# 32x32 block inverses moved by VectorE transposes instead of through DRAM, and an opening in program order, in a DeltaNet and feed-forward kernel

## The chip, the cores and the metric

One core of one Trainium2 chip. The metric is the device time of one execution in microseconds (us). A kernel's time is the median of its runs. A ratio is the mean time of one kernel's fast runs over the mean of the other's fast runs of the same rounds, with a 95% interval, so it isn't quite the ratio of the medians quoted here.

## The reference, cut to what matters

Four batches of eight heads, 768 positions, head width 48: a linear attention whose state is corrected at every position. Its output, 3072 tokens of 384 numbers, goes through a feed-forward network of width 2048.

```python
for t in range(S):
    kt, vt, bt = (k_n[:, :, t], v[:, :, t], beta[:, :, t, None])
    y[:, :, t] = np.einsum('bhd,bhde->bhe', q[:, :, t], state)
    v_old = np.einsum('bhde,bhd->bhe', state, kt)
    state = state + bt[:, :, :, None] * np.einsum('bhd,bhe->bhde', kt, vt - v_old)
...
h = x @ w_in
g = np.maximum(h, 0.0) + alpha * np.minimum(h, 0.0)
return (g @ w_out).astype(np.float32)
```

The kernels cut the sequence into 12 chunks of 64 positions. With two pairs of batches that makes 24 steps. Within a chunk the recurrence is a triangular system of 64x64 for each head, solved with the inverses of its two 32x32 diagonal blocks. VectorE works these out by elimination, one block in each partition ("eliminate"), so a block that lies across 32 partitions has to be moved into one, and its inverse back. The weights arrive as 64-bit words and are turned into fp32 on the chip, piece by piece, by ScalarE, VectorE and GpSimd. A feed-forward "unit" is one chunk's tokens: a first half (times `w_in`, then PReLU) and a second half (times `w_out`).

## The kernel before

The blocks went through DRAM: an image of all blocks was stored, gathered into partitions, and after the elimination stored again and scattered.

```python
def gather(n):
    ...
    nc.sync.dma_start(out=image, in_=kk[n])
    for t in range(2):
        for i in range(2):
            ...
            nc.sync.dma_start(
                out=block[m][blocks_of(n, t, i)],
                in_=image[rows, :, HB * i : HB * i + HB].rearrange("r h c -> h r c"),
            )

def eliminate(m, eng):
    ...                                   # 60 operations on VectorE
    eng.tensor_copy(out=flipped[0:np_], in_=r.rearrange("p r c -> p c r"))
    nc.sync.dma_start(out=inverse[m][0:np_], in_=r)
    nc.sync.dma_start(out=turned[m][0:np_], in_=flipped[0:np_])

def scatter(n):
    ...
    for dst, src, i in (
        (diag[n % NE][first, :, 0:HB], turned[m], 0),
        (diag[n % NE][second, :, HB:C], inverse[m], 1),
        (inv[n % NE][first, :, 0:HB], inverse[m], 0),
    ):
        nc.sync.dma_start(out=dst, in_=src[blocks_of(n, t, i)].rearrange("h r c -> r h c"))
```

The weights' words were converted by one generator, and the order of instructions on each engine was the scheduler's:

```python
for i, (dst, _) in enumerate(pieces):
    ...
    nc.scalar.activation(dst.bitcast(U32), lo, ACT.Copy, scale=2.0**-29)
    nc.scalar.square(size, hi.bitcast(FP32))
    nc.vector...      # two operations: high, hi
    nc.gpsimd.tensor_tensor(out=dst.bitcast(U32), in0=hi, in1=dst.bitcast(U32), op=ALU.add)
    nc.vector...      # one operation: the check
    if i + len(stages) < len(pieces):
        fetch_words(i + len(stages))
```

## Time and profile before

| | kernel before |
|---|---|
| time (median of four runs; 844.66 is that of the three known at the prediction) | 844.2 us |
| the profiled run: time; span | 843.51 us; 841.7 us |
| opening, to the first full pair of steps | 211.9 us, PE busy 118.5 |
| ten pairs of steps | 584.2 us, PE busy 582.3 |
| the last unit | 45.6 us |

The stretch in the middle can be cut once more. The next view of the kernel before gives the busy time by stretches: window, its length, then busy us and number of instructions of PE, PEld, DVE, ACT and POOL, then the granted TensorE clock, the DMA share and GB/s. Steps 4 and 5 are the first line, steps 6 to 23 the second:

```profile
211.90:271.50 59.60, 59.38 (x760) 44.93 (x759) 37.28 (x102) 11.49 (x24) 1.21 (x5) 1.00 0.38 83
271.50:796.10 524.60, 522.89 (x6358) 392.76 (x6358) 217.33 (x567) 94.23 (x186) 4.51 (x22) 1.00 0.25 51
```

In both PE is busy all but 2 us. Whatever helps must act before 212 us, or take work away from PE.

### The profile page before, as it was taken

To read this page: it belongs to the slowest core of one execution; us is meant where nothing else is said; L and a number is where in the kernel's file an instruction comes from. 1 tells how busy PE (TensorE), PEld (TensorE's weight loads), DVE (VectorE), ACT (ScalarE), POOL (GpSimd) and SP (SyncE) were. 2 spreads that over 40 slices of the span, in tenths; PEclk is the share of its full clock that TensorE was granted. 3 is DMA by queue.
4 is the path that set the end of the run, shared out by engine and by line. 5 is a ranking of instruction groups with operands and counts; after the bars stand their busy time and mean duration, and the time that the engine had idled before them with its cause. 6 is when DMAs were issued, how large, how long until landed. Compare 5 with 4: busy or idle time off the path is not lost.

```text
span 841.7 us, 20438 instructions
## 1 busy us (share of the span) xinstructions
PE 742.2 (88%) x8917; PEld 558.1 (66%) x8917; DVE 388.8 (46%) x955; ACT 169.7 (20%) x318; POOL 53.8 (6%) x96
## 2 busy tenths in 40 slices
PE   4402686886999999999999999999999999999997
PEld 3301575653876876867867768768768768677684
DVE  3779764452592430881422943216818713123030
ACT  2231223222211211211302201211212112011010
POOL 5022121122000000000000000000000000000000
PEclk9999989997999999999999999999999999999999
DMA  5774074353325223314303232331333321100000
GB/s 104 196 201 130 18 105 140 102 146 74 72 40 137 46 44 74 58 69 78 66 25 63 59 104 43 57 58 43 85 58 58 61 48 21 23 11 2 20 1 19
DMA packets 178520, 58.06 MB, mean 69 GB/s; under 512 B 167920, under 2 KB 171008, under 8 KB 177664
## 3 DMA queue, kind: packets, MB, share of 16 engines
q1 hardware_dynamic: 177984, 56.65, 30.7%
q8 instruction: 70, 1.15, 0.6%
q10 hardware_dynamic: 448, 0.11, 0.1%
q14 instruction: 18, 0.15, 0.1%
HBM read 39.43 MB, written 17.30 MB: 67 GB/s over the span
## 4 chain that ended last, share of the span: by engine, by line
PE 79%; DVE 8%; issue 6%; POOL 3%; DMA 2%; SPq 1%; ACT 1%; DVEq 0%; POOLq 0%; ACTq 0%
PE p_ffn L536 29%; PE p_ffn L516 28%; PE p_one L464 3%; PE p_one L478 3%; PE p_one L411 3%; PE p_one L422 3%; PE p_big L309 3%; PE p_big L449 2%; PE p_big L282 2%; DVE prod L369 2%; POOL w_out L191 2%; DVE block L375 2%; DMA ke<-in_k_dram 1%; PE p_one L505 1%; PE p_big L484 1%
## 5 line engine op out<-in xcount | busy, mean ns | idle before, releaser
L536 PE MATMUL p_ffn<-w_out,g 128*128 128x384 f32 x768 | 270.2, 500 | 21.5 <-DVE w_out L192 20.5
L516 PE MATMUL p_ffn<-xt,w_in 128*128 128x256 f32 x1152 | 268.2, 386 | 3.1 <-ACT xt L506 2.5
L516 PEld LDWEIGHTS p_ffn<-xt,w_in 128*128 128x128 f32 x1152 | 215.2, 192 | 33.4 <-ACT xt L506 2.8
L536 PEld LDWEIGHTS p_ffn<-w_out,g 128*128 128x128 f32 x768 | 142.7, 193 | 112.4 <-DVE w_out L192 16.7
L527 DVE SCALAR_TENSOR_TENSOR g<-low,al_t,p_ffn 128x256 f32<-128x256 f32 x192 | 85.6, 477 | 130.6 <-ACT low L524 130.3
L524 ACT ACTIVATE low<-p_ffn 128x512 f32<-128x512 f32 x96 | 57.4, 598 | 174.2 <-PE p_ffn L516 165.9
L369 DVE TENSOR_TENSOR prod<-block 128x84 f32<-128x84 f32 (+22 forms) x210 | 70.8, 337 | 5.0
L375 DVE TENSOR_TENSOR block<-block,prod 128x84 f32<-128x84 f32 (+22 forms) x210 | 70.6, 336 | 4.9
L411 PE MATMUL p_one<-diag,kk 64*64 64x32 f32 x768 | 33.2, 226 | 28.4 <-DMA diag<-turned 28.3
L411 PEld LDWEIGHTS p_one<-diag,kk 64*64 64x64 f32 x768 | 29.3, 142 | 39.5 <-issue 37.6
L425 DVE TENSOR_TENSOR inv<-diag,p_one 128x256 f32<-128x256 f32 x24 | 10.1, 419 | 96.1 <-PE p_one L422 84.7
L543 ACT COPY o_sb<-p_ffn 128x384 f32<-128x384 f32 x24 | 11.5, 479 | 169.3 <-PE p_ffn L536 169.3
L452 DVE TENSOR_TENSOR r<-v_raw,p_big 128x384 f32<-128x384 f32 x22 | 12.1, 552 | 72.3 <-PE p_big L449 72.3
L422 PEld LDWEIGHTS p_one<-diag,mid 64*64 64x64 f32 x768 | 25.9, 142 | 13.0 <-ACT mid L414 8.2
L478 PEld LDWEIGHTS p_one<-u,a_t 64*64 64x64 f32 x768 | 25.8, 142 | 11.7 <-issue 8.2
L492 DVE TENSOR_TENSOR y<-y,p_one 128x384 f32<-128x384 f32 x22 | 12.2, 553 | 46.1 <-PE p_one L478 46.1
L422 PE MATMUL p_one<-diag,mid 64*64 64x32 f32 x768 | 28.4, 226 | 4.8 <-ACT mid L414 4.7
L478 PE MATMUL p_one<-u,a_t 64*64 64x48 f32 x768 | 28.9, 227 | 2.0 <-DVE u L466 2.0
L464 PEld LDWEIGHTS p_one<-r,inv 64*64 64x64 f32 x704 | 22.6, 134 | 10.4 <-issue 7.0
L271 POOL TENSOR_TENSOR beta_t<-beta_t,rec 128x8 f32<-128x8 f32 x24 | 7.4, 307 | 345.1 <-DVE rec L269 345.1
L414 ACT COPY mid<-p_one 128x256 f32<-128x256 f32 x24 | 8.9, 372 | 94.1 <-PE p_one L411 94.1
L282 PE MATMUL p_big<-ident,ke 128*128 128x128 f32 x96 | 19.0, 333 | 8.8 <-DMA ke<-in_k_dram 8.7
(78 smaller groups left out, 565.4 us busy)
## 6 DMA issues: line engine op xcount, KB each, us to landing
image<-kk SPq DMA_DIRECT2D x24, 256.0 KB
w_out<-in_moe_w_in_dram SPq DMA_DIRECT2D x6, 1024.0 KB
space<-in_moe_w_out_dram SPq DMA_DIRECT2D x8, 768.0 KB
ke<-in_k_dram SPq DMA_DIRECT2D x48, 96.0 KB
qp<-in_q_dram SPq DMA_DIRECT2D x48, 96.0 KB
v_raw<-in_v_dram SPq DMA_DIRECT2D x48, 96.0 KB
kl<-in_k_dram SPq DMA_DIRECT2D x48, 96.0 KB
out_dram<-o_sb SPq DMA_DIRECT2D x48, 96.0 KB
```

What stands on the lines that cost most here:

```text
L282: nc.tensor.transpose(p[:, g * 128 : (g + 1) * 128], src[:, 2 * g : 2 * g + 2].rearrange("p h d -> p (h d)"), ident,)
L309: nc.tensor.matmul(p[half(t), a, w, g], k_t[n][dims(a), g, half(t)], rhs[n][dims(a), g, half(t)],)
L369: eng.tensor_tensor(out=prod, in0=r[:, 0:j, j : j + 1].to_broadcast([np_, j, n]), in1=r[:, j : j + 1, j + 1 : HB].to_broadcast([np_, j, n] ...
L375: eng.tensor_tensor(out=r[:, 0:j, j + 1 : HB], in0=r[:, 0:j, j + 1 : HB], in1=prod, op=ALU.add)
L411: nc.tensor.matmul(p[half(t), h], kk[n][half(t), h], diag[n % NE][half(t), h, 0:HB])
L422: nc.tensor.matmul(p[half(t), h], mid[n % 2][half(t), h], diag[n % NE][half(t), h, HB:C])
L464: nc.tensor.matmul(p[half(t), h], inv[n % NE][half(t), h], rhs_[n][half(t), h // G, h % G])
L478: nc.tensor.matmul(p[half(t), a, g], a_t[n][half(t), a * G + g], us[n][half(t), a * G + g])
L516: nc.tensor.matmul(p_h[:, i], w_in[:, t, (f + i) * 128 : (f + i + 1) * 128], xt[:, t], start=(t == 0), stop=(t == KT - 1),)
L524: nc.scalar.activation(low, p_h, ACT.Relu, scale=-1.0)
L527: nc.vector.scalar_tensor_tensor(out=g[:, i], in0=low[:, i], scalar=al_t[:, f + i : f + i + 1], in1=p_h[:, i], op0=ALU.mult, op1=ALU.add,)
L536: nc.tensor.matmul(p_o, gs[f // 2][:, f % 2, bp * 128 : (bp + 1) * 128], w_out[:, f], start=(f == 0), stop=(f == FT - 1),)
```

## The change

Its intent: no block goes through DRAM any more; four steps share one elimination from the start (before, the first one served two); the half-empty opening takes more feed-forward work; and the opening's engines follow the order of the source instead of the scheduler's choice. The core of the diff, with cuts:

```diff
+    opening = ExitStack()
+    opening.enter_context(tc.manual_schedule(engines={   # PE, DVE, ACT, POOL, SP
+    ...
-            for dst, src, i in (                          # scatter, gather: gone
-    ...
+        nc.scalar.mul(same[m][:, j], kk[n][:, :, 0:HB], which[:, 0:1])
+        nc.vector.scalar_tensor_tensor(
+            out=same[m][:, j], in0=kk[n][:, :, HB:C], scalar=which[:, 1:2], in1=same[m][:, j],
+            op0=ALU.mult, op1=ALU.add,
+        )
+        if j == NJ - 1:
+            nc.vector.transpose(
+                block[m].rearrange("b r c -> b c r"), same[m].rearrange("r j h c -> r c (j h)")
+            )
     ...
+        nc.vector.transpose(turned[m].rearrange("c b r -> c r b"), r)
+        nc.vector.transpose(inverse[m].rearrange("r b c -> r c b"), r.rearrange("b r c -> b c r"))
     ...
+        nc.scalar.mul(diag[n % NE][:, :, 0:HB], turned[m][:, heads], which[:, 0:1])
+        nc.scalar.mul(diag[n % NE][:, :, HB:C], inverse[m][:, heads], which[:, 1:2])
+        nc.scalar.mul(inv[n % NE][:, :, 0:HB], inverse[m][:, heads], which[:, 0:1])
```

The conversion is cut into parts that the source interleaves with other work. `before` is ScalarE's two copies, `join` VectorE's two operations and GpSimd's addition, `check` VectorE's last:

```diff
+        for i in range(len(pieces) + 1):
+            if i < len(pieces):
+                join(i)
+                yield
+            if i > 0:
+                check(i - 1)
+                if i - 1 + k < len(pieces):
+                    fetch_words(i - 1 + k)
+                    before(i - 1 + k)
+                yield
     ...
+    weave((eliminate(0), HB), (part(conv_in, n_in), n_in))
+    weave((chain(ready(0), pair(0)), READY + PAIR), (part(conv_in, n), n))
+    weave(
+        (chain(ready(2), pair(2)), READY + PAIR), (conv_in, n),
+        (statics(NJ, 2 * NJ - 1), 2 * NJ + 1), (ffn_in(0), IN_PARTS),
+    )
+    weave(
+        (conv_out, PARTS_OUT), (ffn_in(1), IN_PARTS), (statics(2 * NJ, EARLY + 3), ...),
+    )
+    ...
+    weave((eliminate(1), HB), (ffn_out(0, True), OUT_PARTS))
+    ...
+    opening.close()
```

The load of alpha also moves behind all early loads of the one DMA queue.

## The prediction

> **What bounds the kernel now.** I read the page first (slices, chain of waits), then busy time by stretches, then PE's waits in the opening, then the timeline around the first long wait. The slices:
>
> ```profile
> ## 2 busy tenths in 40 slices
> PE   4402686886999999999999999999999999999997
> PEld 3301575653876876867867768768768768677684
> DVE  3779764452592430881422943216818713123030
> ...
> PEclk9999989997999999999999999999999999999999
> DMA  5774074353325223314303232331333321100000
> ```
>
> A slice is 21 us. PE is full from slice 11 on and half idle in the first ten. So there are two kernels: an opening, and a long stretch that TensorE bounds. The stretches (columns: span, then busy us and count of PE, PEld, DVE, ACT, POOL, then granted clock, DMA share, GB/s) put numbers on it:
>
> ```profile
> 0.00:211.90 211.90, 118.52 (x1644) 90.38 (x1644) 127.23 (x270) 57.74 (x98) 48.06 (x69) 0.94 0.51 122
> 211.90:796.10 584.20, 582.27 (x7116) 437.69 (x7116) 254.60 (x669) 105.72 (x210) 5.72 (x27) 1.00 0.27 54
> 796.10:841.70 45.60, 41.36 (x161) 30.05 (x159) 6.97 (x16) 6.21 (x11) 0.00 (x0) 0.99 0.06 13
> ```
>
> After 212 us PE lacks 2 us of 584: nothing there can be won by moving blocks another way, only by giving PE less work. In the opening PE idles 93 of 212 us. Who keeps it waiting there:
>
> ```profile
> PE p_one L411 <- DMA diag<-turned: 28.3, 1, 28.3
> PE p_ffn L536 <- DVE w_out L192: 20.5, 6, 7.6
> PE p_one L464 <- DVE inv L425: 16.4, 1, 16.4
> PE p_big L282 <- DMA ke<-in_k_dram: 8.7, 2, 4.9
> ```
>
> The first wait is the path of the inverted blocks through DRAM, the second the conversion of the 64-bit words of the second weight (VectorE and GpSimd), the third an inverse that stands in VectorE's queue behind the second elimination. The timeline of the first wait:
>
> ```profile
> 49.44 1.03 DVE L381 COPY flipped<-block 64x1024 f32<-64x1024 f32 x1
> ...
> 57.37 0.54 SPq L385 DMA_DIRECT2D turned<-flipped  x1
> ...
> 60.98 0.31 SPq L400 DMA_DIRECT2D diag<-turned  x1
> ...
> 65.80 0.39 PE L411 MATMUL p_one<-diag,kk 64*64 64x32 f32 x2 [28.30 <-DMA diag<-turned]
> ```
>
> The block is inverted by about 48 us, its copies are issued at 57 (they stand in one DMA queue behind key and value loads), scattered from 61, and PE starts at 65.8: 18 us from the last elimination step to use.
>
> **What the skill says.** (1) "VectorE: DVE Perf Modes", section "The three transpose paths": VectorE transposes only within independent 32x32 blocks, SBUF to SBUF. The change cuts its blocks to 32x32, so it fits; no transpose is in this trace. "Vector Engine (DVE) Microarchitecture Reference", section 3.8, says the array sustains one element per cycle per lane. A strided copy of the same 128x1024 took 1.07 us here, so I take 1.2 us per transpose as an estimate. (2) "SBUF — State Buffer", section "SBUF: two separate sides": VectorE and GpSimd share a port pair as an exclusive lock. The trace agrees: of the eight 128x768 shift operations the median took 556 ns and the longest 2116, beginning 0.17 us after a GpSimd add of 1.86 us began. (3) "ScalarE: Activation LUTs", section "What ACT_TABLE_LOAD costs": 186 ns + 0.833 ns per element, and 93 ns more for a per-partition scale. The trace has 518 ns for 384 elements, which fits; the new masked copies of 256 elements are then 0.49 us by estimate.
>
> **The change, part by part.**
>
> Removed: 24 stores of an image, 96 gathers, 14 stores of inverses, 144 scatters, and with them the 18 us above. Per batch, the flipped copy (1.07 us of VectorE) goes. Added per step: one masked copy (0.49, ScalarE), one combine (0.42, VectorE, sized by the 128x256 adds at 0.42), three masked placements (1.5, ScalarE). Added per batch: three transposes, 3.6 us. VectorE so gains about 3.6 - 1.1 + 4 x 0.42 = 4.2 us per batch of four steps, some 25 us in all; ScalarE 48 us in all. In the full stretch VectorE is busy 255 of 584 and ScalarE 106, and the 4 us stand in a pair of steps where VectorE is at 36-37 of 60 us. I count zero for PE there.
>
> Moved: both halves of unit 0 and the first half of unit 1 go into the opening, so steps 4 and 5 are left with half of their feed-forward work. A unit costs PE 96 x 0.216 + 64 x 0.323 = 41.4 us (tail: 20.7 for each half). The pair of steps from 211.9 to 271.5 took 59.6, of which 18.2 is attention. From 271.5 to the end, 570.2 us, the program is the same, as the order of PE's instructions confirms (six steps' lead kept).
>
> The new opening, engines in program order, stage by stage:
> - Loads: alpha is now issued by the one DMA queue behind beta and 18 key, query and value issues. At 0.66 us each, and about 2 for beta, it is issued near 15 and lands near 18 (2.5 us later, as alpha did before). PE's second group of instructions is its transpose, so everything waits: 18, where the old one began at 9-10.
> - Four steps of norms, flips and grams: the old ones took 2.85 us each; with the masked copy about 3. Four of them, a last gram, combine and transpose: 14. Ends at 32.
> - Elimination of four steps at once: mask 1.2, 60 operations averaging 0.337 plus 0.035 between them = 22.3, two transposes 2.4: 26. Ends at 58. PE idles throughout.
> - Steps 0 and 1 with six half pieces of the first weight: VectorE 7 x 1.1 + 5 x 0.7 for the words and 7 for attention, with lock waits for six GpSimd adds of 1.3; ScalarE, in order, waits for each newly fetched piece (0.5 MB, about 4 us). The old pair of attention steps took 27 (90 to 117); I take 27. Ends at 85.
> - Steps 2 and 3, the rest of the first weight, statics 4 to 7 and the first half of unit 0: PE 20.7 + 18.2 + 4.8 = 44. VectorE 11.5 (words) + 8.2 (statics) + 1.2 + 7.9 (attention) + 7 (g) = 36, plus part of 6 GpSimd adds. Two nearly full engines in fixed order: 47. Ends at 132.
> - Second weight with the first half of unit 1: 16 pieces, each 1.45 us of VectorE (0.35 + 0.55 + 0.55, the 768-wide durations scaled) and 0.95 of GpSimd that mostly exclude each other: 38; g 7, two statics 4, part of it under GpSimd: 46. PE needs only 23 here. Ends at 178.
> - Second elimination, 26 us plus a few norms, beside the second half of unit 0: the built order shows 40 source matmuls of 0.645 (two instructions each) before the next inverse is wanted, 26 us. 28. Ends at 206.
> - Steps 4 and 5: 18.2 attention + 24 remaining matmuls x 0.645 = 34, with 3 for filling the chain: 37. Ends at 243.
>
> The old kernel is at 271.5 there, so about 28 us are won. 841.7 - 28.5 = 813 of span; runs take some 3 us longer than the span (844.66 against 841.7): 816 us, 3.4% faster.
>
> **The rivals.** (a) The trip through DRAM is hidden and program order costs what the trip cost. For: the new opening has every engine wait in line; the late alpha costs 8 us, a ScalarE stuck behind a fetch delays copies for PE, and the first elimination now covers four steps with PE idle. Then the stages from 58 to 178 take 140 instead of 120 and the time is 836. Against: the old opening wasted 28 + 20 + 16 us in three named waits, and all three are addressed. (b) VectorE and GpSimd become the bound: if their lock is total, the conversion stages take 28 x 2.7 plus everything else on VectorE, about 15 us more: 830. If GpSimd hides well under g and under PSUM reads, 10 less: 805. (c) Transposes of 4-byte data run far slower than one element per cycle, say 4 us: 5 us more in the opening, 2 x 2.8 x 3 at most on the path: 825 or so, and no effect later, as VectorE has room. (d) The gain also shows in the full stretch because 260 small DMAs vanish. PE's 2 idle us of 584 speak against it: at most 2. (e) The tightest overlap: PE stays nearly busy from 85 on; then 243 becomes 220 and the time 793.
>
> **Range and chances.** Stage errors of 5 to 8 us, partly shared (the lock and the ordering enter two stages), give about 20 either way: 792 to 838. Beyond 2% faster is below 827.8, half a spread above my number: 0.72. Within 2%: 0.25. Slower by over 2% would need an opening 45 us worse than I work out: 0.03.
>
> **What would show it.** Right: transposes at 1.1 to 1.3 us; no wait of PE on a DMA of blocks; PE nearly idle from 32 to 58; alpha as the wait that ends first work near 18; pairs of steps from step 6 at 59 to 61 us and the last stretch of 45.6 unchanged; the start of step 6 near 243. Wrong: PE waits inside the full stretch for placements or eliminations; step 6 beginning at 265 or later (then look which engine stood in line in the second-weight stage); or transposes of several us.

## The result

The changed kernel took 867.79 us (866.61 to 869.64, four runs) against 844.2 for the kernel before: ratio 1.0284, interval 1.0258 to 1.031. Executions over 1.5% slower than the fastest of the same kernel are left out of the means. It is 2.8% slower where 3.4% faster had been predicted, and outside the range. The output is correct.

The profile of the changed kernel, first its slices (21.6 us each), to be held against those of before in the prediction:

```profile
PE   2208596545599998999999999999999999999998
...
PEclk9655699766599999999999999999999999999999
```

PE's thin part is one slice longer than before; slices 8 to 11, at four to five tenths, are new. The granted clock is low there too (five to seven tenths), where before only one slice of the opening was under eight tenths. The stretches, in the columns explained above:

```profile
18.30:36.80 18.50, 9.42 (x153) 7.73 (x153) 10.27 (x22) 9.25 (x21) 1.63 (x8) 0.80 0.86 221
36.80:63.70 26.90, 0.00 (x0) 0.00 (x0) 24.76 (x65) 5.25 (x9) 0.00 (x0) 0.50 0.00 0
63.70:93.20 29.50, 18.92 (x394) 18.21 (x394) 20.18 (x33) 10.77 (x21) 10.64 (x7) 0.56 0.54 122
93.20:151.90 58.70, 47.67 (x780) 39.03 (x779) 34.97 (x73) 20.34 (x46) 8.61 (x13) 0.90 0.28 69
151.90:231.40 79.50, 38.11 (x169) 27.99 (x167) 35.15 (x73) 25.07 (x50) 20.02 (x20) 0.67 0.27 73
231.40:260.00 28.60, 28.60 (x78) 16.17 (x78) 26.54 (x77) 3.94 (x11) 2.31 (x7) 0.89 0.16 32
260.00:297.50 37.50, 37.50 (x814) 28.30 (x814) 20.44 (x47) 12.59 (x28) 0.61 (x3) 1.00 0.27 54
297.50:819.10 521.60, 515.99 (x6366) 389.67 (x6365) 239.33 (x573) 121.20 (x246) 3.96 (x18) 1.00 0.14 28
```

The prediction named a length for each stage, so its lengths can be put beside the measured ones:

| stage | predicted us | measured us |
|---|---|---|
| wait for alpha | 18 | 18.3 |
| statics of four steps, gather transpose | 14 | 18.5 |
| first elimination | 26 | 26.9 |
| steps 0 and 1 | 27 | 29.5 |
| steps 2 and 3, first half of unit 0 | 47 | 58.7 |
| second weight, first half of unit 1 | 46 | 79.5 |
| second elimination, second half of unit 0 | 28 | 28.6 |
| steps 4 and 5 | 37 | 37.5 |
| step 6 to 23 | 524.6 (as before) | 521.6 |

The opening ends at 297.5, not at 243. Of the 54.5 us, 33.5 arise in the stage of the second weight. What is odd in its line: in 79.5 us PE worked 38, VectorE 35, ScalarE 25 and GpSimd 20. No engine is full. Who kept PE waiting in the first 300 us:

```profile
PE p_one L440 <- ACT q_t L343: 31.9, 1, 31.9
PE p_ffn L547 <- DVE g L558: 31.2, 6, 8.9
PE p_one L279 <- DMA al_sb<-in_moe_alpha_dram: 9.9, 1, 9.9
...
PE p_one L324 <- DMA kl<-in_k_dram: 5.7, 1, 5.7
```

The first is the wait over the first elimination, which the prediction had expected. The second wasn't expected at all: the matmuls of unit 1 wait for the PReLU of the unit itself (`g`), which frees one of the two PSUM tiles that they write. The chain of waits around one such wait (start, length, what was waited for or done) shows why:

```profile
161.64 3.98 DMA space_out<-in_moe_w_out_dram
...
165.64 0.55 ACT w_out L190
...
166.22 0.54 ACT space_out L192
166.76 0.49 ACT low L555
...
167.67 0.47 DVE g L558
168.15 0.28 DVE high L199
...
168.93 0.55 DVE w_out L214
169.48 1.10 DVE high L199
...
170.61 0.56 DVE space_out L203
171.17 0.48 DVE w_out L214
171.65 0.02 SPq L179
...
171.71 3.02 DMA space_out<-in_moe_w_out_dram
```

Read it from the top. A fetch of words lands. ScalarE's two conversion copies (L190, L192) had been standing on it; only behind them in ScalarE's queue comes `low`, the Relu of unit 1, whose input was long ready (PE had stood still since 159.4). VectorE makes `g` from it and goes on with the words. At 171.2 it begins a check, and that check is what allows the next fetch; when the check ends, 0.5 us later, the fetch is issued, and ScalarE's next copy needs what it brings, 3 us later, with the next Relu behind it. ScalarE's sum of such waits (us, times, longest):

```profile
ACT w_out L190 <- DMA space_out<-in_moe_w_out_dram: 42.1, 11, 7.5
```

So the source line that issues a fetch and, in the same breath, the copies that need it, puts the whole latency of a fetch on ScalarE, and with it on unit 1. That was a reading of one trace, and the next section tests it.

### The profile page after: what moved, and what is told of

Same layout as the page of the kernel before. It is cut to its first block, busy times and chain, and to the rows that moved or that the text cites. A ratio compares the mean times of both kernels' runs of the same rounds, so it can differ in the third digit from the quotient of the medians.

```text
span 864.8 us, 20260 instructions
## 1 busy us (share of the span) xinstructions
PE 739.1 (85%) x8917; PEld 558.6 (65%) x8917; DVE 420.8 (49%) x977; ACT 216.1 (25%) x442; POOL 57.0 (7%) x108
## 4 chain that ended last, share of the span: by engine, by line
PE 61%; DVE 24%; DMA 5%; ACT 4%; SPq 3%; issue 3%; POOL 0%; ACTq 0%; DVEq 0%
PE p_ffn L576 24%; PE p_ffn L547 20%; DVE block L414 6%; DVE prod L408 6%; DMA space_out<-in_moe_w_out_dram 3%; DVE g L558 3%; PE p_one L507 2%; PE p_one L493 2%; PE p_one L440 2%; PE p_big L354 2%; PE p_one L451 2%; PE p_big L478 2%; SPq L111 2%; DVE block L394 1%; DVE turned L419 1%
## 5 line engine op out<-in xcount | busy, mean ns | idle before, releaser
L547 PE MATMUL p_ffn<-xt,w_in 128*128 128x256 f32 x1152 | 283.2, 399 | 41.8 <-DVE g L558 34.6
L547 PEld LDWEIGHTS p_ffn<-xt,w_in 128*128 128x128 f32 x1152 | 221.3, 198 | 79.6 <-issue 37.9
L576 PE MATMUL p_ffn<-w_out,g 128*128 128x384 f32 x768 | 263.5, 495 | 4.7 <-DVE g L558 2.4
L558 DVE SCALAR_TENSOR_TENSOR g<-low,al_t,p_ffn 128x256 f32<-128x256 f32 x192 | 83.4, 477 | 155.4 <-ACT low L555 155.3
L408 DVE TENSOR_TENSOR prod<-block 128x30 f32<-128x30 f32 (+9 forms) x180 | 59.3, 330 | 5.5
L414 DVE TENSOR_TENSOR block<-block,prod 128x30 f32<-128x30 f32 (+9 forms) x180 | 59.4, 330 | 5.0
L440 PE MATMUL p_one<-diag,kk 64*64 64x32 f32 x768 | 27.8, 225 | 31.9 <-ACT q_t L343 31.9
L440 PEld LDWEIGHTS p_one<-diag,kk 64*64 64x64 f32 x768 | 26.0, 142 | 33.0 <-issue 32.1
L481 DVE TENSOR_TENSOR r<-v_raw,p_big 128x384 f32<-128x384 f32 x22 | 12.0, 551 | 39.2 <-PE p_big L478 39.0
L307 DVE TENSOR_REDUCE norm<-ksq 128x8 f32<-128x384 f32 x24 | 13.2, 548 | 32.1 <-ACT ksq L305 32.1
L507 PE MATMUL p_one<-u,a_t 64*64 64x48 f32 x768 | 28.3, 225 | 0.0
L493 PE MATMUL p_one<-r,inv 64*64 64x48 f32 x704 | 25.0, 220 | 0.0
```

The lines of the kernel that those rows point to most:

```text
L408: nc.vector.tensor_tensor(out=prod, in0=r[:, 0:j, j : j + 1].to_broadcast([128, j, n]), in1=r[:, j : j + 1, j + 1 : HB].to_broadcast([128, ...
L414: nc.vector.tensor_tensor(out=r[:, 0:j, j + 1 : HB], in0=r[:, 0:j, j + 1 : HB], in1=prod, op=ALU.add)
L440: nc.tensor.matmul(p[half(t), h], kk[n][half(t), h], diag[n % NE][half(t), h, 0:HB])
L493: nc.tensor.matmul(p[half(t), h], inv[n % NE][half(t), h], rhs_[n][half(t), h // G, h % G])
L507: nc.tensor.matmul(p[half(t), a, g], a_t[n][half(t), a * G + g], us[n][half(t), a * G + g])
L547: nc.tensor.matmul(p_h[:, i], w_in[:, t, (f + i) * 128 : (f + i + 1) * 128], xt[:, t], start=(t == 0), stop=(t == KT - 1),)
```

## The experiments

Twelve kernels ran. Where nothing else is said the kernel is the changed one with one edit and gives a correct result. "The stage" is the one of the second weight, from ScalarE's first copy of that weight to the mask of the second elimination; by this measure it is 80.6 us in the changed kernel.

### late: ScalarE's copies one check later

```diff
                     fetch_words(i - 1 + k)
-                    before(i - 1 + k)
+                if i > 1 and i - 2 + k < len(pieces):
+                    before(i - 2 + k)
```

> Only the place of ScalarE's first two copies of a piece moves: at each check they take the piece fetched one check earlier, not the one fetched just now. Theory A (the second-weight stage is a chain of just-issued fetch, ScalarE stuck in line on it, the Relu copy behind it, g, next check; 79.5 us against the 46 worked out): the stage from 152 to 231 falls to 50-58 us, PE's waits for g there from 31 us in total to under 12, and the time to 838-848. Rival B (VectorE and GpSimd exclude each other and bound that stage): it stays at 75-80, time 864-868. Rival C (the data itself comes too slowly for three slots): stage 70-78, time 860-866.

839.72 us (837.99 to 842.21), ratio to before 0.9945 (0.9915 to 0.9974): 28 us less than the changed kernel. The stage by stretches:

```profile
150.62:208.55 57.93, 37.23 (x175) 27.47 (x174) 35.25 (x75) 25.90 (x52) 20.27 (x20) 0.76 0.35 98
```

It fell from 80.6 to 57.9 with the same work in it, and PE's wait for `g` from 31.2 to 14.5; 22.6 of the 24.4 us between the two profiled spans lie here. One moved call is worth 3% of the whole kernel, and rivals B and C, which kept the stage above 70, are out. The wait didn't sink below 12 as expected: ScalarE still stands 27.1 us on fetches, since one check later is often less than 3 us later.

### loads: alpha early, no second load of the fourth key block

```diff
+    al_sb = work.tile([FT, 128], FP32, name="al_sb", tag="ksq", bufs=1)
+    nc.sync.dma_start(out=al_sb, in_=moe_alpha.rearrange("(f p) -> f p", p=128))
     for n in range(1, NKE + 1):
         load_early(n)
     ...
-            load_early(n + NKE)
+            if n > 0:
+                load_early(n + NKE)
```

> Alpha is loaded right behind beta, and the fourth key block isn't loaded a second time. Theory: the first PE work after beta, now at 18.3 us, starts near 9 to 10, and the 2.4 us wait for the second copy of the fourth key block goes; the loads for keys then pace the first steps; 6 to 10 us less, time 858-862. Rival (the first weight's pieces, which come later in the same queue, become the wait instead): under 3 us less.

853.3 us (852.2 to 854.34), ratio 1.0112: 14.5 us less, and better than expected. The gather transpose begins at 21.3 instead of 34.7, so both load orders together cost 13.4 us there, and nothing of it is lost later. The prediction had counted alpha's lateness but not the second load, which queues behind 3 MB of words and lands after 8.3 us.

### free: the same source, the order left to the scheduler

```diff
-    opening.enter_context(tc.manual_schedule(engines={ ... }))
```

> Only the program order of the opening is taken away; the scheduler orders it as in the kernel before. If fixed order causes the loss: the second-weight stage falls to about 50 us and the steps 2-3 stage to about 48, time 825-840. If the loss lies in the dependences themselves (slots, lock, elimination of four steps at once with PE idle), the time stays within 10 us of 867.

817.9 us (817.08 to 818.42), ratio 0.9692: 50 us less than with program order, better than expected. PE now has one long wait,

```profile
L436 PE MATMUL p_one<-diag,kk 64*64 64x32 f32 x768 | 27.6, 224 | 58.4 <-ACT diag L425 58.4
```

(line, engine, tiles and count, busy us and mean ns, idle us ahead of it and what ended it): the scheduler mixes the first elimination with the conversion of the words on VectorE, so the elimination ends near 99 us instead of 64. It still wins. By then the first weight and eight of the second's sixteen pieces are converted, and from 97 to 250 us PE is busy 147 of 153 us.

### blocks: the kernel before with nothing but the transposes

The kernel before, its own batches and its own scheduler; `gather`, the copy `flipped` and `scatter` replaced by the masked copies and transposes of the change.

> The kernel before with one part of the change: blocks moved by transposes and masked copies, its own batches, scheduler and opening kept. Theory (the transposes themselves are a gain in the opening and next to none later): the 28 us wait of PE for a placed block falls to about 12, the full stretch loses about 4 us in all, time 822-836. Rival (transposes at 2 us and ScalarE's masked copies cost what the trip cost): 840-850. If it is slower than 850 the block path itself is the loss.

807.0 us (806.65 to 807.98), ratio 0.9565 (0.9543 to 0.9588): 37 us faster than the kernel before, better than expected, and not by the mechanism expected. Its stretches and PE's waits in the opening:

```profile
0.00:177.94 177.94, 113.59 (x1629) 88.07 (x1629) 143.46 (x285) 69.09 (x124) 47.64 (x75) 0.96 0.43 112
177.94:759.40 581.46, 576.60 (x7132) 435.98 (x7131) 287.82 (x693) 136.86 (x280) 7.06 (x28) 1.00 0.15 29
```

```profile
PE p_one L409 <- ACT diag L398: 36.7, 2, 35.7
PE p_ffn L534 <- DVE w_out L189: 6.3, 4, 2.3
```

The cut is at the same piece of work as in the kernel before, the first matmul of the second unit, which began there at 211.8. So 34 of the 37 us lie in the opening, 177.9 against 211.8. The long stretch is 2.8 us shorter, 581.5 against 584.3, with some 280 small DMAs gone; PE itself was busy 6 us less there for about the same number of matmuls, and no run shows why. PE's wait for the first blocks has not become shorter but longer, 36.7 against 28.3, because it is now a wait for the elimination, mixed with words on VectorE. What vanished are the other two: the 16.4 us for an inverse are gone, and the 20.5 for words of the second weight are 6.3. So taking the trip through DRAM out pays at the second batch and the second weight, more than at the first block. Which of the freed things does it, the DMA queue or VectorE's order, these runs don't separate.

### warm: TensorE kept busy through the first elimination

28 dummy matmuls of 128x384 were woven into the first elimination, to lift the granted clock from 0.50.

> The changed kernel with 28 idle-time multiplications of 128x384 on TensorE during the first elimination; nothing reads them. Rival D (the low granted clock, 0.50 to 0.67 in the opening, is what makes the change slow): with TensorE kept busy the clock stays up, and the stages after lose 15 to 25 us; time 842-852. My theory (TensorE is not what these stages wait for): the stage of steps 0 and 1, 29.5 us, loses 2 to 5, the second-weight stage nothing; time 860-866.

866.63 us (865.28 to 868.08), ratio 1.0269: as the changed kernel. The stretch of the first elimination now reads

```profile
36.80:63.70 26.90, 16.49 (x57) 9.84 (x55) 24.73 (x65) 5.77 (x10) 0.00 (x0) 0.86 0.00 1
```

with a clock of 0.86 instead of 0.50, and the stage of the second weight still took 79.3 us. A low clock ahead of the stages is not the cause. The clock inside the second-weight stage was 0.72 against 0.67, so this run alone doesn't exclude an effect there. late does better: PE was busy 37.2 us in its stage (clock 0.76) against 39.2 (0.67), while the stage lost 22.6 us. Nor does the time follow the clock from run to run: the four runs of free, with mean clocks of 0.944 to 1.0, took 817.1 to 818.4 us.

### one_unit: no feed-forward work beside the second weight

The first half of unit 1 was taken out of the opening and done later, as an ordinary unit.

> The changed kernel without the first half of unit 1 in the opening; it goes back beside steps 4 and 5. If the second-weight stage is a chain of fetch, ScalarE and g, then without the Relu copies and g in the line it falls from 79.5 to 50-58 us, TensorE gets 20.7 us more work later, and the time is 861-868: no gain from the move, about no loss either. If the move as such costs (g on VectorE next to the words), the time falls under 855. If the move paid, it rises over 872.

865.16 us (864.4 to 870.74), ratio 1.026. The stage is short, but its work comes back later:

```profile
150.86:206.21 55.35, 7.40 (x81) 5.58 (x82) 30.63 (x60) 21.80 (x44) 20.71 (x20) 0.51 0.34 102
```

55.4 us with PE busy for 7.4. Without unit 1 the conversion alone still needs 55 us in this order. Putting the unit's 20.7 us of PE work beside it lengthens it by 25, so the opening gained nothing from that work: it might as well have been done later. In program order, that is the part of the intent that failed.

### nofetch: the later pieces of the second weight not fetched

```diff
-                    fetch_words(i - 1 + k)
+                    if len(pieces) < 16:
+                        fetch_words(i - 1 + k)
```

Wrong result (relative error 1.88): the last 13 pieces are converted from what lies in their space.

> Wrong result on purpose: the second weight's later 13 pieces are not fetched, the stale words are converted again; all else as in the changed kernel, program order included. It tells how much of the 80.6 us of the second-weight stage is waiting for fetches. Theory A with fetch as the whole cause: the stage falls to 46-50 us, time 832-838. If VectorE, GpSimd and ScalarE in fixed order also cost (the later copies left 57.9 us): 52-57 us, 840-846. If fetches are no cause: over 75.

836.61 us (835.83 to 839.36), ratio 0.9903. The stage:

```profile
155.17:205.56 50.39, 30.50 (x175) 22.73 (x174) 37.62 (x76) 24.66 (x52) 19.96 (x20) 0.89 0.09 17
```

50.4 us with unit 1 in it. Without the fetch the stage is 4 us above the 46 predicted; with it, 80.6. The two runs together say it clearly: the words without the unit take 55, the words and the unit without the fetch 50, and all three in one ScalarE queue 81.

### nofetch_in: the same for the first weight

> The changed kernel, program order kept, but of the first weight only the six half pieces loaded ahead are fetched; the later six are converted from what lies in the space (wrong result on purpose; the second weight is fetched as in the changed kernel). In the stages of steps 0 to 3 ScalarE stood 17.2 us on five fetches of the first weight. If standing on the fetch is also what made the stage of steps 2 and 3 take 58.7 us instead of the 47 predicted, the two stages together, 88.2 us in the changed kernel, fall to 74 to 79 and the time to 854 to 858. If the excess of that stage is the fixed order itself (copies for TensorE behind conversions, conversions behind attention) and the fetch lies beside it, they fall by at most 5 us and the time is 862 to 867.

Wrong result (relative error 0.71). 859.65 us (858.76 to 860.53), ratio 1.0179: between the two expectations. The stages of steps 0 to 3 together are 81.2 us (from 63.7 to 144.9) instead of 88.2. So 7 us of the 14 by which these two stages missed their prediction are fetches; the cause of the other 7 is not shown. The trace of the changed kernel has candidates in the fixed order (4.15 us of PE for a check of the first weight that stood behind the gather transpose on VectorE, 2.65 for a GpSimd addition), which no run took away one by one.

### late_loads, free_ll and hybrid: the repairs together, with and without program order

late_loads is late and loads together, in program order. free_ll is the same with the scheduler's order. hybrid was meant to keep program order to the end of the first elimination and leave the rest to the scheduler:

```diff
     weave((eliminate(0), HB), (part(conv_in, n_in), n_in))
+    opening.close()
     ...
-    opening.close()
```

> Program order kept, with both edits: the later ScalarE copies (839.7 alone) and the early alpha with no second key load (853.3 alone). The two lie in different stages of a serial opening, so they add: 867 - 27 - 14 = 826, within 823-830. If they overlap, 836-840.

> The changed kernel without program order, with the later ScalarE copies, alpha early and the second load of the fourth key block gone. The scheduler's order of the changed opening took 817.9 us; alpha early takes 8 us from its start, the later copies little, as the scheduler isn't stuck in line: 805-812. If the scheduler puts the words ahead of the elimination again, 815-818.

> Both edits, and program order only up to the end of the first elimination, the scheduler after it. The first elimination ends near 50 us instead of 70 (scheduler alone, 798.6), since no words are put between its operations; but those words come later, on a VectorE that is then nearly full. If TensorE's start counts: 785-794. If VectorE's sum of work counts: 796-806.

| kernel | median us (range) | ratio to before (interval) |
|---|---|---|
| late_loads | 826.54 (825.38 to 826.79) | 0.9775 (0.9742 to 0.9808) |
| free_ll | 798.61 (796.59 to 799.83) | 0.9455 (0.9431 to 0.948) |
| hybrid | 798.23 (797.27 to 800.06) | 0.9439 (0.9401 to 0.9477) |

The two repairs nearly add up: 28.1 and 14.5 alone, 41.3 together. Program order costs 28 us even in the repaired source (826.5 against 798.6). hybrid does not show where, because its first elimination did not stay in program order. VectorE's timeline has the words between its operations (`prod` and `block` are the elimination):

```profile
37.87 0.37 DVE L415 TENSOR_TENSOR block<-block,prod 128x220 f32<-128x220 f32 x1
38.17 1.77 DVE L214 SCALAR_TENSOR_TENSOR w_in<-w_out,w_in 128x512 f32<-128x512 f32 x1
39.87 0.38 DVE L409 TENSOR_TENSOR prod<-block 128x228 f32<-128x228 f32 x1
```

It ended at 73.8 us, as in free_ll (73.5), and not near 50 as expected. So hybrid is nearly free_ll once more, and that the two take the same time doesn't settle whether order or sum counts on VectorE. The other traces do place the loss. In late_loads, which kept the order, the first elimination ended at 50.2 us, and PE began with its blocks at 51.7, 20.6 us earlier than in free_ll (72.3); its span is 29.7 us longer all the same (824.5 against 794.8). So program order loses some 50 us after the first elimination, in part because free_ll had converted words during it.

free_ll and hybrid beat the kernel before by 5.5% and the changed kernel by 8%. Against blocks, which has the transposes alone (807.0 us), they gain only 1% more.

### blocks_fine: blocks with smaller pieces of the weights

`W_IN_P = 512` and `W_OUT_T = 1` in blocks, the piece sizes of the change.

> The kernel with blocks alone moved by transposes (807.0 us), with the weights in half pieces as in the change. Finer pieces let VectorE's elimination pass between words, 2 to 6 us less: 800-806. Rival: twice as many operations with their fixed cost, on a VectorE that is nearly full from 20 to 80 us: 808-815.

805.55 us (801.67 to 805.73), ratio 0.9529 (0.9565 for blocks in the same kind of rounds). The size of the pieces is worth little: under half a per cent.

## Why the prediction was wrong

The prediction said 816 us and faster; it was 868 and slower. By its own steps:

- **What bounds the kernel: right.** Little was to be won in the long stretch: steps 6 to 23 took 521.6 us against 524.6, and the last 45.7 are unchanged. It allowed "at most 2" there and it was 3 (2.8 in blocks).
- **The trip through DRAM: right in sign, too small in size.** No wait on a DMA of blocks is left. By itself this part is worth 37 us (blocks), more than the 28 that the prediction gave the whole change.
- **Transposes: mis-sized.** "I take 1.2 us per transpose": they took 1.95 to 2.06. This is the view of the instruction groups of the changed kernel (columns as above):

```profile
L394 DVE STREAM_TRANSPOSE block<-same 128x1024 f32<-128x1024 f32 x6 | 12.3, 2058 | 0.2
L421 DVE STREAM_TRANSPOSE inverse<-block 128x1024 f32<-128x1024 f32 x6 | 12.0, 2006 | 0.0
```

  On the path of the opening that is about 2.5 us for three of them; rival (c) was the right worry at a smaller size, though its own sum (5, then 2 x 2.8 x 3 = 17 at most, then 825) doesn't add up. The masked copies (0.50 to 0.51 us against 0.49) and the combine (0.485 against 0.42) fit.
- **Loads: a term left out.** Alpha's landing near 18 was right. The second load of the fourth key block was not seen, and the statics took 18.5 us for 14. What the two load orders cost the time is 14.5 us (loads).
- **Second weight with the first half of unit 1: the step that failed.** The prediction summed 38 + 7 + 4 and took 3 off for overlap with GpSimd, 46 us, as if the only limit were the work of VectorE and GpSimd: "PE needs only 23 here." (PE was busy 38, as one matmul of unit 1 took 541 ns at a clock of 0.67, against 424 in nofetch at 0.89; but it was idle another 41.) It had named the danger for the first weight ("ScalarE, in order, waits for each newly fetched piece") and then counted no fetch for the second. The sum of work was nearly right: without fetches the stage took 50.4. What took its place is a loop through the DMA queue, ScalarE and VectorE: check, fetch of 3 to 4 us, two copies, Relu, PReLU, next check. ScalarE stood 42.1 us on fetches. One call moved (late) brings 23 us of the stage back, no fetch (nofetch) 30, no unit (one_unit) 25.
- **Steps 2 and 3: mis-sized.** 58.7 for 47. About half of what steps 0 to 3 were over is fetches of the first weight (nofetch_in); for the other half the trace has only candidates.
- **The rivals.** Rival (a), "program order costs what the trip cost", was the right one, at 836 and as a minor case. Program order costs 50 us (free), more than the trip brings. The lock of VectorE and GpSimd (b) is there, as in `high` of 1.10 us in the chain, which takes 0.35 alone, but it was already in the 38; GpSimd's additions, put at 0.95 us, took 1.18. The clock, which the prediction didn't consider, fell too but is not the cause (warm, late). "An opening 45 us worse than I work out: 0.03" was too sure: eight stages with one common assumption, that queues stand in line only for work, are not eight independent errors. A small slip besides: the profiled run took 1.8 us more than its span (843.51 against 841.7), not 3, since 844.66 is of another run.

Open: why the granted clock falls to 0.50 in the changed kernel and not in the kernel before, what the remaining 7 us of steps 0 to 3 are one by one, whether order on VectorE matters in the first elimination (hybrid failed to test it), and whether blocks gains through the freed DMA queue or through VectorE's order.

## What to carry to other kernels

When instructions keep the order of the source, an instruction that needs a transfer must not be written next to the line that starts the transfer: its engine stands there until the data land (3 to 4 us a piece here), and everything written behind it, needed or not, stands too. Sum work per engine for a bound, but then follow one round of each loop through all engines and add the latencies; where no engine is full and the stage is long, such a loop is the first thing to look for. And test the parts of a bundled change alone: here one part was worth 37 us and another cost 50, and the sum looked like a small loss.

## What the Trainium skill lacked or had wrong

- "Vector Engine (DVE) Microarchitecture Reference", section 3.8, has the transpose sustain one element per cycle per lane. The fp32 32x32 transposes of 128x1024 with strided operands took 1.95 to 2.06 us, while a strided copy of the same size took 1.07 in the kernel before: about half the rate of a copy. Whether 4-byte data or the strides do it, no run separates.
- "PSUM — Partial Sum Buffer", section "Engine vs sequencer instructions", says that the queues of ScalarE, VectorE and GpSimd are strict FIFO. The traces agree, but the page doesn't draw the consequence: a copy placed just behind its own fetch held ScalarE 42.1 us in one stage and cost 28 us of 868.
- "TensorE: Matmul & The Clock Gate", "Part 1: The HAM clock gate", has the clock at half rate by default and after an idle window. The record agrees for the changed kernel (0.50 over 26.9 us without a matmul) and not for the kernel before (1.00 from 50.5 to 65.8 us, PE busy 0.00), nor for free (1.00 from 40 to 64 us, PE busy 1.13 of 24). From 42 to 64 us PE was busy 0.00 in free_ll and in hybrid; the record says 0.50 in one and 1.00 in the other, and their times differ by 0.4 us. Keeping PE busy there raised the record to 0.86 and changed the time by 0.1%.
